# Query scores in a fused agent attention: agents as fp32 weights, softmax by 32x32 turns on VectorE

## The chip, the cores and the metric

The kernel runs on one core of one Trainium2 chip. The metric is the time of one execution in microseconds (us), the median of several runs. Besides these, one execution was recorded by the hardware profiler; all rows shown are from it. Engines are TensorE (PE in the profile, with PEld its weight loads), VectorE (DVE), ScalarE (ACT), GpSimd (POOL) and SyncE (SP, which issues DMAs).

## The reference

Four batches of 12480 tokens with 128 channels, 49 agents per batch, then a gated feed-forward layer with 2048 hidden columns over all 49920 tokens:

```python
def sm(a, b):
    s = scale * (a @ b.transpose(0, 2, 1))
    s = s - s.max(-1, keepdims=True)
    e = np.exp(s)
    return e / (e.sum(-1, keepdims=True) + 1e-09)
a2k = sm(agents, k)          # 49 x 12480 per batch
agent_v = a2k @ v            # 49 x 128
q2a = sm(q, agents)          # 12480 x 49
x = (q2a @ agent_v)          # 12480 x 128
h = x @ w_in                 # 128 -> 2048
out = (h * (1 / (1 + np.exp(-1.702 * h)))) @ w_out
```

The weights of the feed-forward layer come as float64.

## The kernel before

`agent_v @ w_in` is worked out once per batch, so that the up product of a token is its 49 softmax values times a 49 x 2048 matrix (`wh`, `wl`: the high part in fp32r and the rest). The tokens go in 52 **groups** of 960 (`GT`), 13 a batch; a group is held as two halves of 480 tokens, half c on the partitions from 64c on. For a group there are 16 **chunks** of 128 hidden columns (`NF`). A chunk has three pairs of up matmuls (`up`, L538: wh x q_hi, wh x q_lo, wl x q_hi, one of each pair per row tile of 64 rows), a gelu on ScalarE (L558), the high part gh of it (by a GpSimd DMA for even chunks and chunks 1 and 9, else on ScalarE), the rest gl on VectorE (`low`, L575), and six pairs of down matmuls (`down`, L580), in two rounds of three, since each row tile adds to both output banks `po`. All of these go through `half_matmul` (L209), where two row tiles run side by side.

The order on every engine is written out by hand. A group is 17 **gaps** (`GAPS`); each gap first runs the jobs put into it (`at[t]`, in the order of the `put` calls), then the up pairs of a chunk (six chunks ahead of its down matmuls), then gl of the chunk three before that, then the second down round of one chunk and the first of the next. Gap 1 has no up pairs (L1039), so that 17 gaps hold 16 chunks. At the end of a group `store` (L603) copies the two output banks out: both halves on ScalarE for the first five groups of the first three batches, else one on ScalarE and one on VectorE.

The next group's softmax stands in these gaps (L902 to L917). Before them, in gaps 12 to 15 of the group before, VectorE splits q into three bf16 parts (`split`, L185, four pieces). In gaps 0 and 1 `scores` (L230) multiplies them with bf16 parts of the agents, 16 pairs of small matmuls a run, tokens as weights, with the two runs swapping the banks of `ps_m`; the result has 120 tokens on the partitions. In gap 2 `query_shift` (L461) adds two sums, takes the maximum and subtracts it; gap 4 has the exp on ScalarE (with a table load before and after), gap 6 the sums and the product (L486, L492), gap 8 the transposes of `query_pairs` (L501) on TensorE, from which ScalarE and VectorE make q_hi and q_lo.

Keys and values of the next batch take slots in the same gaps (L939 on): key scores at gaps 4, 10 and 13 of a group, each with four split pieces before it and a store on ScalarE and VectorE after it; values at gaps 12 and 6, each with a DMA, a subtraction (L369), a sum (L391) and a pair of operations on e (L361). `ps_m` is one buffer of two PSUM banks, shared by all of them.

The start (`start`, L784) handles the first batch's keys and values in fp32, with the first two groups' scores (`scores_exact`) and their softmax between the steps of the key softmax on VectorE; then `first_weights` (L400) copies the accumulated values and the first up matmuls follow. Its value matmuls (`first_values`, L763) are fp32 on column tiles: 49 weights of 64 columns, at `tile_position=(0, c * H)`.

Of the kernel before, what the change touches and what calls it, by code (L numbers as in the profile page):

```python
# [17 lines left out]
P = 128  # L18
# [11 lines left out]
Z_AT = 6  # L30
P_AT = 8
# [10 lines left out]
def kernel(  # L42
# [31 lines left out]
    ag_sb = const.tile([P, B, A], F32, name="ag_sb")  # L74
    nc.sync.dma_start(out=ag_sb, in_=agT)
# [19 lines left out]
    p_pad = const.tile([P, CH // TB, P], F32, name="p_pad")  # L95
    nc.gpsimd.memset(p_pad, 0.0)


    e_sb = const.tile([P, KB, A + 1], F32, name="e_sb")
    nc.gpsimd.memset(e_sb[:, :, A:], EPS)  # L100
# [70 lines left out]
    rest = ag_sb  # L171
# [84 lines left out]
    def scores_exact(b, x, out):  # L256

        for j in range(KB):
            nc.tensor.matmul(
                out=out(j), lhsT=x[:, j * TB : (j + 1) * TB], rhs=ag_sb[:, b, :], start=True, stop=True  # L260
            )
# [22 lines left out]
    def first_key_scores(g, kt):  # L284

        for c in range(2):
            ps = ps_h.tile([P, 512], F32, name="ph")
            for j in range(KB // 2):
                nc.tensor.matmul(  # L289
                    out=ps[:TB, j * 2 * A : (j + 1) * 2 * A],  # L290
                    lhsT=kt[:, c * KB // 2 + j, :],
                    rhs=ag_sb[:, 0:2, :].rearrange("p b a -> p (b a)"),
                    start=True,
                    stop=True,
                )
# [160 lines left out]
    def query_load(b, g):  # L456
        t = loads.tile([P, GT + PAD], F32, name="qt", tag="qt", bufs=1)
        nc.sync.dma_start(out=t[:, 0:GT], in_=qT[b, :, g * GT : (g + 1) * GT])
        return t

    def query_shift(s):  # L461

        m = work.tile([P, KB], F32, name="m")
        sd = e_sb[:TB, :, 0:A]
        if isinstance(s, tuple):
            nc.scalar.copy(out=by_bank(sd), in_=s[0])
            nc.vector.tensor_add(out=by_bank(sd), in0=s[1], in1=by_bank(sd))
            s = [by_bank(sd)]
        mb = m[:TB].rearrange("p (c j) -> p c j", c=2)
        at = 0  # L470
        for bank in s:
            c = slice(at, at + bank.shape[1])
            at = c.stop
            nc.vector.tensor_reduce(out=mb[:, c], in_=bank, axis=AX.X, op=ALU.max)
            nc.vector.tensor_tensor(
                out=by_bank(sd)[:, c],
                in0=bank,
                in1=mb[:, c].unsqueeze(3).broadcast_to([TB, c.stop - c.start, KB // 2, A]),
                op=ALU.subtract,
            )  # L480
        return sd
# [4 lines left out]
    def query_sums(n):  # L486
        z = work.tile([P, KB], F32, name="z")
        nc.vector.tensor_reduce(out=z[:TB], in_=e_sb[:TB], axis=AX.X, op=ALU.add)
        nc.vector.reciprocal(out=z[:TB], in_=z[:TB])
        return z  # L490

    def query_softmax(n, e, z):  # L492
        pp = p_pad
        nc.vector.tensor_tensor(
            out=pp[:TB].rearrange("p i (c x) -> p c i x", c=2)[:, :, :, 0:A],
            in0=e.rearrange("p (c i) a -> p c i a", c=2),
            in1=z[:TB].rearrange("p (c i) -> p c i", c=2).unsqueeze(3).broadcast_to([TB, 2, KB // 2, A]),
            op=ALU.mult,
        )

    def query_pairs(g):  # L501
        pp = p_pad
        ps = two_banks()
        q_hi = work.tile([P, CH], F32R, name="q_hi")
        q_lo = work.tile([P, CH], F32R, name="q_lo")
        r = slice(0, H + A)
        rows = [slice(0, H), slice(H, TB)]
        for i in range(CH // TB):
            for c, t in enumerate(rows):
                n = t.stop - t.start  # L510
                half_matmul(
                    (ps.name, c),
                    c,
                    out=ps[:, c, i * n : (i + 1) * n],
                    lhsT=pp[t, i, :],
                    rhs=ident[t, t],
                    start=True,
                    stop=True,
                    is_transpose=True,
                )  # L520

        def piece(q, c):
            t = rows[c]
            return q[r].rearrange("p (i t) -> p i t", t=TB)[:, :, t]

        def scored(c):
            n = rows[c].stop - rows[c].start
            return ps[r, c, : CH // TB * n].rearrange("p (i t) -> p i t", t=n)

        for c in range(2):  # L530
            nc.scalar.copy(out=piece(q_hi, c), in_=scored(c))
        for c in range(2):
            nc.vector.tensor_sub(out=piece(q_lo, c), in0=scored(c), in1=piece(q_hi, c).bitcast(F32))
# [92 lines left out]
    q_parts = {}  # L626
# [32 lines left out]
    def do_query_split(n, i):  # L659
        if n in exact:  # L660
            q_parts[n] = qts.pop(n, None) or q_parts[n]
        elif n < B * NG:
            if i == 0:
                q_parts[n], pieces[n] = split(qts.pop(n))
            pieces[n](i)

# [14 lines left out]
    def do_key_sum(b, g):  # L681
        if g == 0:
            accs[b] = work.tile([P, 2, 2 * C + 1], F32, name="acc")
        key_sum(g, sums.pop((b, g)), accs[b])

    def do_query_scores(n, c):
        if n < B * NG:
            if c == 0:
                banks[n] = score_banks() if n in exact else wide_banks()
            if n not in exact:  # L690
# [430 lines left out]
```

## Time and profile before

| | |
|---|---|
| median of three runs | 1903.03 us (1902.35 to 1903.81) |
| the profiled execution's span, first to last instruction | 1901.8 us |
| TensorE busy | 1887.1 us (99%) |
| VectorE busy | 1547.8 us (81%) |
| ScalarE busy | 1431.9 us (75%) |
| GpSimd busy | 327.7 us (17%) |
| chain of waits that ended last, by engine | PE 86%, issue 7%, DMA 2%, DVE 2% |

The span is that of the profiled execution; the runs' times lie about 1.2 us above it. Matmuls overlap, so their durations add up to more than the time that they take: what a stretch of them costs is read from the starts of its neighbours. In a row such as `128x480 f32<-128x480 f32` the first shape is the output, the second the input.

### The profile page before, as it was taken

The numbers are of one execution on the slowest core, as the hardware profiler recorded it, in microseconds if no ns is written. First come the engines' busy times: TensorE is split into PE (matmuls) and PEld (weight loads), VectorE is DVE, ScalarE is ACT, GpSimd is POOL, SyncE is SP. The second block draws the span as 40 slices with busy tenths as digits, with TensorE's granted clock in tenths as the row PEclk, the third lists the DMA queues.
The fourth block names the chain that finished last, engine by engine and source line by source line (L and its number), as shares of the span: only waits on it lengthen the run. The fifth ranks groups of instructions, "written<-read, shape, count | busy, mean of one in ns | idle before, by whom it ended". The sixth has DMA issues, their size and how long they took to land.

```text
span 1901.8 us, 53518 instructions
## 1 busy us (share of the span) xinstructions
PE 1887.1 (99%) x22152; PEld 1767.2 (93%) x22152; DVE 1547.8 (81%) x2042; ACT 1431.9 (75%) x2480; POOL 327.7 (17%) x671
## 2 busy tenths in 40 slices
PE   8999999999999999999999999999999999999999
PEld 8799999999899999999988999999898999999998
DVE  7888889788789888888878898888887777777775
ACT  4777777778777777777777777877777878778785
POOL 0111112222111111222211111222211111111111
PEclk9999999999999999999999999999999999999999
DMA  9566478888566657978856655999984555555453
GB/s 355 181 204 204 167 215 227 223 231 231 165 202 216 199 170 221 224 225 231 220 166 215 197 187 175 222 228 227 224 207 153 191 174 178 178 185 179 168 185 137
DMA packets 158863, 384.57 MB, mean 202 GB/s; under 512 B 15683, under 2 KB 73219, under 8 KB 158619
## 3 DMA queue, kind: packets, MB, share of 16 engines
q0 software_dynamic: 115008, 273.33, 48.0%
q1 hardware_dynamic: 43611, 107.83, 19.8%
q8 instruction: 173, 2.83, 0.7%
q14 instruction: 71, 0.58, 0.1%
HBM read 82.25 MB, written 25.56 MB: 57 GB/s over the span
## 4 chain that ended last, share of the span: by engine, by line
PE 86%; issue 7%; DMA 2%; DVE 2%; POOL 1%; ACT 1%; SPq 0%; POOLq 0%; DVEq 0%; ACTq 0%
PE po L213 49%; PE ph L213 26%; PE ps_m L213 7%; DMA gh<-g 2%; PE ph L289 1%; DVE gl L577 1%; PE ps_m L425 1%; POOL gh L570 1%; DMA vt<-v 1%; PE po L599 0%; ACT g L558 0%; POOL v_pair L365 0%; PE po L769 0%; DMA kt<-kT 0%; ACT L558 0%
## 5 line engine op out<-in xcount | busy, mean ns | idle before, releaser
L558 ACT ACTIVATE g<-ph 128x480 f32<-128x480 f32 x1664 | 853.7, 571 | 372.7 <-PE ph L213 359.9
L577 DVE TENSOR_TENSOR gl<-g,gh 128x960 fp32r<-128x960 f32 x832 | 940.0, 1153 | 170.4 <-DMA gh<-g 136.9
L213 PE MATMUL po<-gh,wo_h 64*128 64x480 f32 x3300 | 795.1, 380 | 2.7 <-SPq L220 2.7
L213 PE MATMUL po<-gl,wo_h 64*128 64x480 f32 x3300 | 788.4, 377 | 0.1
L213 PE MATMUL po<-gh,wo_l 64*128 64x480 f32 x3300 | 787.4, 376 | 0.0
L570 POOL DMA_DIRECT2D gh<-g x517 | 275.9, 534 | 1521.8 <-ACT g L558 1275.8
L213 PEld LDWEIGHTS po<-gh,wo_h 64*128 64x128 f32 x3300 | 464.3, 184 | 20.1 <-ACT o L607 4.3
L213 PEld LDWEIGHTS po<-gl,wo_h 64*128 64x128 f32 x3300 | 465.5, 186 | 13.4 <-DVE gl L577 1.5
L213 PEld LDWEIGHTS po<-gh,wo_l 64*128 64x128 f32 x3300 | 463.5, 184 | 12.7
L213 PE MATMUL ph<-q_hi,wh 49*128 49x480 f32 x1664 | 417.8, 400 | 1.0 <-ACT g L558 0.8
L213 PE MATMUL ph<-q_lo,wh 49*128 49x480 f32 x1664 | 397.3, 377 | 0.0
L213 PE MATMUL ph<-q_hi,wl 49*128 49x480 f32 x1664 | 395.6, 376 | 0.0
L572 ACT CAST gh<-g 128x960 fp32r<-128x960 f32 x312 | 312.7, 1002 | 8.3
L213 PEld LDWEIGHTS ph<-q_hi,wh 49*128 49x128 f32 x1664 | 233.7, 185 | 21.3 <-ACT g L558 9.2
L213 PEld LDWEIGHTS ph<-q_hi,wl 49*128 49x128 f32 x1664 | 232.6, 184 | 7.8 <-DVE wl L431 0.6
L213 PEld LDWEIGHTS ph<-q_lo,wh 49*128 49x128 f32 x1664 | 233.5, 187 | 4.9
L213 PE MATMUL ps_m<-ag_part,rest 64*128 64x98 bf16 (+1 forms) x2816 | 135.9, 192 | 0.1
L194 DVE TENSOR_TENSOR rest<-rest 128x488 bf16<-128x488 f32 (+1 forms) x176 | 127.3, 724 | 0.0
L213 PEld LDWEIGHTS <-rest 64*128 64x128 bf16 x2816 | 122.7, 94 | 0.3
L213 PE MATMUL ps_m<-ag_part,qt 64*128 64x98 bf16 (+1 forms) x1600 | 81.3, 195 | 0.0
L213 PEld LDWEIGHTS <-qt 64*128 64x128 bf16 x1600 | 66.9, 93 | 14.0 <-issue 9.2
L609 DVE COPY o<-po 128x480 f32<-128x480 f32 x37 | 24.3, 658 | 56.7 <-PE po L213 51.2
(130 smaller groups left out, 1331.8 us busy)
## 6 DMA issues: line engine op xcount, KB each, us to landing
gh<-g POOLq DMA_DIRECT2D x517, 480.0 KB, 3.8
kt<-kT SPq DMA_DIRECT2D x52, 480.0 KB, 4.1
outT<-o SPq DMA_DIRECT2D x104, 240.0 KB, 4.8
qt<-qT SPq DMA_DIRECT2D x50, 480.0 KB, 4.2
vt<-v SPq DMA_DIRECT2D x39, 512.0 KB, 4.7
v_pair<-vt POOLq DMA_DIRECT2D x39, 480.0 KB, 6.6
vt<-v SPq DMA_DIRECT2D x13, 480.0 KB, 4.8
words<-w_in SPq DMA_DIRECT2D x4, 512.0 KB, 8.7
```

What stands on the lines that cost most here:

```text
L194: nc.vector.tensor_sub(out=halves(r)[1][:, s], in0=r[:, s], in1=halves(r)[0][:, s])
L213: ins = nc.tensor.matmul(tile_position=(c * H, 0), **kw)
L289: nc.tensor.matmul(out=ps[:TB, j * 2 * A : (j + 1) * 2 * A], lhsT=kt[:, c * KB // 2 + j, :], rhs=ag_sb[:, 0:2, :].rearrange("p b a -> p (b ...
L425: nc.tensor.matmul(out=out, lhsT=w["avT"], rhs=w_in_sb[:, s], start=True, stop=True)
L558: nc.scalar.activation(out=g[:, c, :], in_=ph[c][:, :CH], func=AF.Gelu_apprx_sigmoid)
L570: nc.gpsimd.dma_start(out=gh, in_=g)
L572: nc.scalar.copy(out=gh, in_=g)
L577: nc.vector.tensor_sub(out=gl, in0=g, in1=gh.bitcast(F32))
L609: nc.vector.tensor_copy(out=o, in_=po[c][:, :CH])
```

## The change

The scores of a group are made with the agents as weights, in fp32: four matmuls, 64 weights (49 agents, then 15 of them again) by 240 tokens, two on each of two column tiles; agents then lie on the partitions and tokens stream. VectorE turns the result in blocks of 32x32, so that a token's 64 values lie in two blocks on two sets of 32 partitions; it takes maximum and sums over both (`other_agents` copies the neighbour's small tile across), and turns back after the product. The splits of q, the second run, the pads and the transposes on TensorE go. Gap 0 is now the one without up pairs, and sums, product and q_hi, q_lo stand in gaps 5, 6 and 7.

```diff
-Z_AT = 6
-P_AT = 8
+Z_AT = 5
+P_AT = 6
+R_AT = 7
+BL = 32
...
+    ag_raw = gpool.tile([P, B, A], F32, name="ag_raw", tag="gl", bufs=GL_BUFS)
+    nc.sync.dma_start(out=ag_raw, in_=agT)
+    ag_sb = const.tile([P, B, H], F32, name="ag_sb")
+    nc.vector.tensor_copy(out=ag_sb[:, :, 0:A], in_=ag_raw)
+    nc.vector.tensor_copy(out=ag_sb[:, :, A:], in_=ag_raw[:, :, BL : BL + H - A])
...
+    def query_scores(b, x, ps):
+        n = CH // 2
+        for i in range(2):
+            for c in range(2):
+                t = c * CH + i * n
+                nc.tensor.matmul(
+                    out=ps[c * H : (c + 1) * H, i * n : (i + 1) * n],
+                    lhsT=ag_sb[:, b, :],
+                    rhs=x[:, t : t + n],
+                    start=True,
+                    stop=True,
+                    tile_position=(0, c * H),
+                )
+    def other_agents(t):
+        x = work.tile([P, CH // BL], F32, name="x", bufs=1)
+        for i in range(0, P, BL):
+            to = i ^ BL
+            nc.vector.tensor_copy(out=x[to : to + BL], in_=t[i : i + BL])
+        return x
+    def query_turn(ps):
+        e = work.tile([P, CH], F32, name="e")
+        nc.vector.transpose(out=e, in_=ps[:, :CH])
+        return e
+    def query_shift(e):
+        m = work.tile([P, CH // BL], F32, name="m", bufs=1)
+        nc.vector.tensor_reduce(out=m, in_=blocks(e), axis=AX.X, op=ALU.max)
+        x = other_agents(m)
+        nc.vector.tensor_tensor(out=m, in0=m, in1=x, op=ALU.max)
+        nc.vector.tensor_tensor(out=blocks(e), in0=blocks(e), in1=per_block(m), op=ALU.subtract)
+    def query_sums(e):
+        n = A - BL
+        z = work.tile([P, CH // BL], F32, name="z", bufs=1)
+        r = work.tile([P, CH // BL], F32, name="r", bufs=1)
+        nc.vector.tensor_reduce(out=z, in_=blocks(e)[:, :, 0:n], axis=AX.X, op=ALU.add)
+        nc.vector.tensor_reduce(out=r, in_=blocks(e)[:, :, n:BL], axis=AX.X, op=ALU.add)
+        nc.vector.scalar_tensor_tensor(out=z, in0=r, scalar=low_rows[:, 0:1], in1=z, op0=ALU.mult, op1=ALU.add)
+        x = other_agents(z)
+        nc.vector.scalar_tensor_tensor(out=z, in0=x, scalar=EPS, in1=z, op0=ALU.add, op1=ALU.add)
+        nc.vector.reciprocal(out=z, in_=z)
+        return z
+    def query_softmax(e, z):
+        nc.vector.tensor_tensor(out=blocks(e), in0=blocks(e), in1=per_block(z), op=ALU.mult)
+        p = work.tile([P, CH], F32, name="p", tag="e")
+        nc.vector.transpose(out=p, in_=e)
+        return p
+    def query_pairs(p):
+        q_hi = work.tile([P, CH], F32R, name="q_hi")
+        q_lo = work.tile([P, CH], F32R, name="q_lo")
+        nc.scalar.copy(out=q_hi, in_=p)
+        nc.vector.tensor_sub(out=q_lo, in0=p, in1=q_hi.bitcast(F32))
         return q_hi, q_lo
...
         if n:
-            for i in range(4):
-                put(t - 5 + i, lambda m=m, i=i: do_query_split(m, i))
-            take(t, 2)
-            put(t, lambda m=m: do_query_scores(m, 0))
-            put(t + 1, lambda m=m: do_query_scores(m, 1))
-            put(t + 2, lambda m=m: do_query_shift(m))
+            take(t, 1)
+            put(t, lambda m=m: do_query_scores(m))
+            put(t + 1, lambda m=m: do_query_turn(m))
             put(t + E_AT, lambda m=m: do_query_exp(m))
             put(t + Z_AT, lambda m=m: do_query_sums(m))
-            put(t + Z_AT, lambda m=m: do_query_softmax(m))
-        take(t + P_AT, 1)
-        put(t + P_AT, lambda m=m: do_query_pairs(m))
+            put(t + P_AT, lambda m=m: do_query_softmax(m))
+        put(t + R_AT, lambda m=m: do_query_pairs(m))
...
-        elif n == 0 and k < 2:
-            u = LAG - 1 + k
         elif final:
             u = n * NF + LAG + k
-        elif k == 1:
-            u = None
+        elif k == 0:
+            u = LAG - 1 if n == 0 else None
         else:
-            u = n * NF + LAG + max(k - 1, 0)
+            u = n * NF + LAG + k - 1
```

`do_query_turn` runs `query_turn` and `query_shift` one after the other. In the start the calls stay where they were: the scores of both groups by `query_scores`, their shift, sums and product by the new functions.

## Rows read from the trace of the kernel before

**Rows 1.** The page's busy time of each engine: us, share of the span, instructions.
```profile
PE 1887.1 (99%) x22152; PEld 1767.2 (93%) x22152; DVE 1547.8 (81%) x2042; ACT 1431.9 (75%) x2480; POOL 327.7 (17%) x671
```

**Rows 2.** Key, value, plain group: length, PE PEld DVE ACT POOL busy, clock, DMA.
```profile
1000.79:1038.09 37.30, 37.28 (x554) 33.33 (x553) 33.65 (x48) 27.64 (x49) 5.78 (x14) 1.00 0.61 199
423.27:458.31 35.04, 35.04 (x396) 34.53 (x393) 29.03 (x37) 27.16 (x47) 7.37 (x14) 1.00 0.86 228
1603.45:1636.63 33.18, 33.18 (x363) 30.84 (x360) 24.32 (x29) 26.15 (x46) 5.96 (x12) 1.00 0.53 180
```

**Rows 3.** Timeline of TensorE around both score runs: start, us, line, output<-input, count.
```profile
1603.24 0.56 PE L213 MATMUL po<-gh,wo_l 64*128 64x480 f32 x2
...
1604.40 0.49 PE L213 MATMUL ph<-q_lo,wh 49*128 49x480 f32 x2
...
1605.28 0.48 PE L213 MATMUL po<-gh,wo_l 64*128 64x480 f32 x2
...
1606.38 0.49 PE L213 MATMUL po<-gl,wo_h 64*128 64x480 f32 x2
```

**Rows 4.** Timeline of TensorE around the transposes, and ten steady pairs after.
```profile
1619.14 0.57 PE L213 MATMUL po<-gh,wo_l 64*128 64x480 f32 x2
...
1619.88 0.57 PE L213 MATMUL ph<-q_lo,wh 49*128 49x480 f32 x2
...
1622.05 0.58 PE L213 MATMUL ph<-q_hi,wl 49*128 49x480 f32 x2
```

**Rows 5.** Timeline of TensorE: fp32 on column tiles, and one full-array fp32 matmul.
```profile
33.06 4.61 PE L769 MATMUL po<-vt,score 120*49 120x129 f32 x80
...
49.07 1.09 PE L769 MATMUL po<-vt,score 120*49 120x129 f32 x16 [0.41 <-DMA vt<-v]
...
72.61 0.38 PE L213 MATMUL po<-gh,wo_l 64*128 64x480 f32 x2
72.92 1.12 PE L425 MATMUL ps_m<-w_in_sb,avT 128*128 128x512 f32 x2
...
74.30 0.38 PE L213 MATMUL ph<-q_lo,wh 49*128 49x480 f32 x2
```

**Rows 6.** VectorE's groups by line and shape: count, busy us, mean ns, idle before.
```profile
L194 DVE TENSOR_TENSOR rest<-rest 128x488 bf16<-128x488 f32 x88 | 64.0, 727 | 0.0
...
L474 DVE TENSOR_REDUCE m<-e_sb 120x8 f32<-120x392 f32 x50 | 28.1, 562 | 1.7
...
L609 DVE COPY o<-po 128x480 f32<-128x480 f32 x37 | 24.3, 658 | 56.7 <-PE po L213 51.2 <-PE po L599 5.3
...
L489 DVE RECIPROCAL z<-z 120x8 f32<-120x8 f32 x52 | 10.6, 203 | 1.8
...
L173 DVE CAST ag_part<-ag_sb 128x196 bf16<-128x196 f32 x1 | 1.8, 1795 | 1.8 <-DMA ag_sb<-agT 1.8
```

**Rows 7.** Timeline of the start: the first key scores, VectorE's first and last query work.
```profile
5.42 22.73 PE L289 MATMUL ph<-ag_sb,kt 128*120 128x98 f32 x208 [0.17 <-DMA kt<-kT]
...
33.04 0.56 DVE L474 TENSOR_REDUCE m<-ps_m 120x8 f32<-120x392 f32 x1
...
46.98 0.57 DVE L494 TENSOR_TENSOR p_pad<-e_sb,z 120x392 f32<-120x392 f32 x1
50.19 0.29 DVE L402 COPY both<-po 128x130 f32<-128x130 f32 x1 [2.65 <-PE po L769]
```

**Rows 8.** Timeline after a group's end: the output's copies and the first down weights.
```profile
1038.55 1.03 ACT L607 COPY o<-po 128x480 f32<-128x480 f32 x2
...
1039.63 0.18 PEld L213 LDWEIGHTS po<-gh,wo_h 64*128 64x128 f32 x1 [0.27 <-ACT o L607]
```

**Rows 9.** Timeline of a value group: gl of chunk 9, and its first use.
```profile
442.10 1.16 DVE L577 TENSOR_TENSOR gl<-g,gh 128x960 fp32r<-128x960 f32 x1 [3.20 <-DMA gh<-g]
443.18 0.72 DVE L533 TENSOR_TENSOR q_lo<-ps_m,q_hi 113x256 fp32r<-113x256 f32 x2
...
443.77 0.46 PE L213 MATMUL po<-gl,wo_h 64*128 64x480 f32 x2
```

More of the change, by code (lines that the diff above doesn't have):

```diff
@@ L259, in scores_exact @@
             nc.tensor.matmul(
-                out=out(j), lhsT=x[:, j * TB : (j + 1) * TB], rhs=ag_sb[:, b, :], start=True, stop=True
+                out=out(j), lhsT=x[:, j * TB : (j + 1) * TB], rhs=ag_sb[:, b, 0:A], start=True, stop=True
             )
@@ L456, in query_load @@
     def query_load(b, g):
-        t = loads.tile([P, GT + PAD], F32, name="qt", tag="qt", bufs=1)
-        nc.sync.dma_start(out=t[:, 0:GT], in_=qT[b, :, g * GT : (g + 1) * GT])
-        return t
[L461 to L481, printed above, removed]
+        t = loads.tile([P, GT], F32, name="qt", tag="qt", bufs=1)
@@ new lines, in query_load @@
+        nc.sync.dma_start(out=t, in_=qT[b, :, g * GT : (g + 1) * GT])
+        return t
+    def query_scores(b, x, ps):
+        n = CH // 2
+        for i in range(2):
+            for c in range(2):
+                t = c * CH + i * n
[7 more added lines that the diff above has]
+                )
@@ L522, in piece @@
[L522 to L533, printed above, removed]
+        nc.scalar.copy(out=q_hi, in_=p)
@@ L625 @@
     k_parts = {}
-    q_parts = {}
     scored = {}
@@ L657, in do_key_split @@
         pieces[b, g](i)
[L659 to L665, printed above, removed]
     def do_key_scores(b, g, c):
@@ L682, in do_key_sum, with do_query_scores, do_query_turn @@
         if g == 0:
-            accs[b] = work.tile([P, 2, 2 * C + 1], F32, name="acc")
+            accs[b] = work.tile([P, 2, 2 * C + 1], F32, name="acc", bufs=1)
         key_sum(g, sums.pop((b, g)), accs[b])
-    def do_query_scores(n, c):
+    def do_query_scores(n, ps=None):
         if n < B * NG:
-            if c == 0:
-                banks[n] = score_banks() if n in exact else wide_banks()
-            if n not in exact:
-                scores(n // NG, q_parts[n], banks[n][0], c, True)
-            elif c == 0:
-                scores_exact(n // NG, q_parts[n], columns(banks[n][0]))
-    def do_query_shift(n):
+            banks[n] = two_banks()[:, 0] if ps is None else ps
+            query_scores(n // NG, qts.pop(n), banks[n])
+    def do_query_turn(n):
         if n < B * NG:
-            s = banks.pop(n)[1]
-            scored[n] = query_shift(s if isinstance(s, (list, tuple)) else [s])
+            scored[n] = query_turn(banks.pop(n))
+            query_shift(scored[n])
     def do_query_exp(n):
@@ L705, in do_query_sums @@
         if n < B * NG:
-            sums[n] = query_sums(n)
+            sums[n] = query_sums(scored[n])
     def do_query_softmax(n):
         if n < B * NG:
-            query_softmax(n, scored.pop(n), sums.pop(n))
+            scored[n] = query_softmax(scored[n], sums.pop(n))
     def do_query_pairs(n):
         if n < B * NG:
-            pairs[n] = query_pairs(n)
+            pairs[n] = query_pairs(scored.pop(n))
     def first_keys():
@@ L810, in start @@
                     steps.pop(0)()
-        banks[0] = score_banks()
-        scores_exact(0, qts.pop(0), columns(banks[0][0]))
+        do_query_scores(0)
         d = {}
@@ L818, in start @@
         key_max_2(d, ps_h.tile([P, 512], F32, name="ph"))
-        halves1 = [ps_h.tile([P, 512], F32, name="ph") for _ in range(2)]
-        scores_exact(0, qts.pop(1), lambda j: halves1[j // 4][:TB, j % 4 * A : (j % 4 + 1) * A])
-        banks[1] = None, [
-            t[:TB, : KB // 2 * A].rearrange("p (c j a) -> p c j a", c=1, a=A) for t in halves1
-        ]
+        do_query_scores(1, ps_h.tile([P, 512], F32, name="ph"))
         for g in range(NKG):
@@ L885, in gap_of @@
         n, k = divmod(u - LAG, NF)
-        return LAG + n * GAPS + (k + 1 if k else 0)
+        return LAG + n * GAPS + k + 1
     def put(t, fn):
```

51 lines of the change are left out of this document (11 added, 40 removed).

## The prediction

> **What bounds the kernel now.** I read the busy times first. TensorE is busy 1887.1 us of 1901.8 [rows 1]; the other engines have room. Then three groups cut out of the steady part, each from the start of one group's query scores to the next [rows 2]: one in which the next batch's keys are scored (three key runs), one in which keys meet values, one with neither. [...] The reader is to see two things: time taken from TensorE's stream is time gained, and VectorE has little left in the key groups. By the code there are 39 key tiles after the first batch, scored three a group, and 39 value tiles, two a group: some 13 key groups and 20 value groups of 52.
>
> **Part 1: TensorE's stream.** A steady pair of row-tile matmuls takes 0.217 us: ten pairs from 1619.88 to 1622.05 [rows 4]. What a query run costs is the time between the pair before and the pair after, less one pair. First run: 1603.24 to 1604.40 holds one pair of wo_l, the run, one pair of q_hi whose second start is late: 1.16 - 0.43 = 0.73. Second run: 1605.28 to 1606.38, 1.10 - 0.43 = 0.67. Transposes of the finished softmax: 1619.14 to 1619.88, 0.74 - 0.43 = 0.31 [rows 3, 4]. Together 1.71. The other way round, the group's 33.18 us less 144 pairs (16 chunks of nine) is 33.18 - 31.25 = 1.93, which holds a few small hitches as well. I take 1.75 removed per group.
>
> Added: four fp32 matmuls of 240 columns, two on each column tile, each of which runs as two passes. The nearest rows are the start's value matmuls, fp32 on the same two column tiles [rows 5]: 80 passes take 4.61 us and 16 take 1.09, so 64 passes take 3.52, or 0.110 for two passes of 129 columns; that is 0.853 ns a column for two passes. The full-array fp32 matmul below needs 1.25 us for 1024 columns of one pass, so at 0.43 ns a column and pass the two tiles can only run side by side. Eight passes of 240 columns are four such steps of 0.205, 0.82 us. The change of tile shape costs more: a 512-column fp32 matmul between row-tile pairs, 72.61 to 74.30, takes 1.69 - 0.43 = 1.26, of which its two passes at 0.853 ns are 0.87; 0.39 are edges. With weights half as wide the edges are somewhat shorter; I take 0.35. New run: 1.17 (bounds 1.05 to 1.30 with tiles side by side, 2.0 if they are not). Gain 1.75 - 1.17 = 0.58 a group, times 50 groups, 29.0; the transposes of the second group, which has its scores in the start, add 0.3. **Minus 29.3** (bounds minus 38 and minus 22).
>
> **Part 2: the cover of the output banks.** The new group's first down matmul waits until the last group's output has been copied out of its two banks. Where ScalarE does both copies (groups 0 to 4 of the first three batches, 15 times) it begins at 1038.55, 0.46 after the group's start at 1038.09, and the second bank's weight load goes at 1039.63, 0.27 late: 1.54 after the start [rows 8]. Now the run is followed by that down matmul at once, since the gap has no up matmuls: TensorE is there at 1.17 and not at about 1.3. It waits some 0.2 longer, 15 times: **plus 3** (0 to 6). In the other groups one copy is on VectorE and both are done near 1.0, which the run just covers.
>
> **Part 3: VectorE.** Removed per group: four split pieces of at most 0.73, five passes of 392 columns at 0.56, a reciprocal of 0.20, two subtractions of some 0.8 together: 6.6. Added [rows 6]: by 562 ns for 392 columns and 658 for 480 an operation costs 1.09 ns a column and 0.13. Turn, maximum and subtraction of the shift are 0.66 each, with four copies of 15 columns and one maximum of two small tiles: the trace has 0.20 for 8 columns where the operation waits for the one before (L489), and neighbours that don't wait overlap by 0.08 (442.10 + 1.16 against 443.18 [rows 9]), which would make it 0.1; I take 0.2 for each since every such chain begins and ends with a wait: 3.0. Sums: 0.41 + 0.38 for 17 and 15 of 32 columns, four copies and three more small ones: 2.2. Softmax and turn back 1.4, q_lo 0.66. Together 7.2 us, 0.6 more than before. The trace has no turn on VectorE: 0.66 is what an operation of 480 columns out of PSUM takes (L609), and twice that is the other bound.
>
> [...]
>
> [...]
>
> *In the start* VectorE is the bound. Its work from the first query operation at 33.04 to the last, ending at 47.55, is without a pause; then it is idle 2.65 us before it copies the accumulated values at 50.19, from which the first weights, and with them every up matmul, follow [rows 7]. All of both groups' query work stands ahead of that copy. Per group it is now some 3.3 and will be 7.2: 2 x 3.9 = 7.8, less the 2.65: **plus 5.2** (3.3 to 7.8). The new copies of the agents ahead of the first key scores are hidden: the agents land at about 2.75, even a copy as slow as the cast there (1.80) and a second of 0.2 end by 4.8, and the first key tile lands only at 5.4 [rows 6, 7].
>
> *In the steady part* the order counts, since each gl must be there when its down pair comes. Gaps without other work last 1.95 (nine pairs); a gap's first wo_h pair of chunk f needs gl three gaps after it was issued, seven pairs into the gap. Counted from the scores' start: gap 0 is 1.17 + 0.65, so chunk 3 is wanted at 7.2. VectorE can begin the turn at 1.4, ends the shift at 4.4, then a key piece of 0.7 and gl of chunk 3, done at 6.3: in time by 0.9, where before it came ahead of the shift. Going on with 1.1 a gl and 0.7 a piece, the sums end at 12.8, the softmax at 15.2, key store and piece at 16.9, gl of chunk 8 at 18.0 (wanted 18.3), of chunk 9 at 20.3 (wanted 20.3). After that no query split stands in gaps 12 to 15 any more and VectorE catches up. So a key group stalls by nothing to half a microsecond; I take 0.1. In a value group the tight one is chunk 9, today held by its DMA and not by VectorE's load: 3.20 us idle until 442.10, done at 443.26, used at 443.77 [rows 9], a slack of 0.5. TensorE will be there 0.58 + 0.3 earlier, the DMA only by the 0.3 that the stream gains ahead of it: 0.1 late from that alone, and if VectorE's own backlog counts (two gl, 3.0 shift, 0.9 key pair, 2.2 sums, 1.4, then q_lo, key sum and pair ahead of chunk 9) about 1.0 late. I take 0.4 of these. 13 x 0.1 + 20 x 0.4: **plus 9.3** (0 to 33, a full microsecond in each of the 33).
>
> ScalarE loses a copy and gains nothing of size. Its q_hi now comes one gap earlier and waits for VectorE's turn back; I cost that at nothing because the exp in gap 4 puts ScalarE itself behind at that point. If that cover is gone it waits up to a gap, and TensorE has two chunks of ph ahead of it to go on with. GpSimd loses 50 memsets of pads. The key slots, the loads and the gap in which exp stands are as before.
>
> **Sum.** 1901.85 - 29.3 + 3 + 5.2 + 9.3 = 1890.0. The median of the runs, 1903.03, lies 1.2 above the span; with it 1891.2.
>
> **The rivals.**
> - *VectorE is never late.* The small copies cost 0.1, chunk 9's DMA moves with the stream: the 9.3 go and half of part 2. 1880. For it: VectorE is idle 3.6 us even in the key group, and the added work is only 0.6. Against: the work moves into the first seven gaps.
> - *VectorE becomes the bound in key and value groups* (the other side). Place: the gl behind shift, sums and softmax. Price: if a turn takes 1.3 rather than 0.66 and a small copy 0.3, the chain up to chunk 9 is 2.1 longer (0.64 twice and 0.1 eight times), so the 33 groups lose some 1.9 each, 63 us instead of 9.3: 1945. It decides from a loss of (29.3 - 5.2 - 3) / 33 = 0.64 us per group on. For it: idle time of 3.65 and no slack by my own count. Against: gl catches up in each group's last gaps.
> - *The column tiles run one after the other*, because both take 128 rows. The run is 2.0, 0.25 worse than what it replaces: 1903.0 + 12.2 + 5.2 + 3 = 1923. Against it stand the start's matmuls at 120 rows [rows 5].
>
> **How the numbers follow.** Forecast 0.50, VectorE never late 0.25, VectorE the bound 0.15, tiles in turn 0.05, else 0.05. A measurement of this kernel can tell 0.2%, 3.8 us, from no change. The forecast's own bounds run from 1871 to 1926 if all terms go one way; three quarters of its chance is below 1899, an eighth within. Faster: 0.375 + 0.25 + 0.02 = 0.65; same 0.10; slower 0.25. The range 1874 to 1912 reaches into the first rival whole and leaves the far part of the others out; the likeliest case alone is 1880 to 1903.
>
> **What would show it.** Score pass pairs 0.2 us apart and a run of 1.1 to 1.2 between pairs; a plain group of 32.6 us against 33.18; the copy of the accumulated values near 55.4 in place of 50.19; VectorE's turn at 0.66; TensorE waiting for gl in the gaps 8 to 10 of value groups. Wrong if the run is over 1.5, if a turn is over 1 us, or if ScalarE is seen waiting for the turn back for more than a microsecond a group.

## The result and the profile after

The changed kernel takes 1929.88 us (median of 4 runs, 1926.15 to 1930.66), the kernel before 1903.42 on the same chip: ratio 1.0133, 95% interval 1.0119 to 1.0147. It is slower by 1.3%; the prediction, 1891.2 with a range of 1874 to 1912, has the wrong sign. The profiled execution has a span of 1928.7 us against 1901.8.

The page of the changed kernel, busy time of each engine (answers to [rows 1]) and its chain that ended last, by engine:

```profile
PE 1886.9 (98%) x18920; PEld 1658.0 (86%) x18920; DVE 1576.5 (82%) x2468; ACT 1417.8 (74%) x2378; POOL 320.9 (17%) x623
...
PE 68%; DVE 14%; issue 8%; ACT 3%; DMA 2%; POOL 1%; SPq 0%; POOLq 0%; DVEq 0%; ACTq 0%
```

TensorE is busy for as long as before (1887.1), in a span that is 26.9 longer: it now waits. VectorE, which had 2% of the chain before, has 14%. The groups of the changed kernel, from one score run to the next (answers to [rows 2]): a key group, two value groups, a plain group; length, then busy PE, PEld, DVE, ACT, POOL, clock, DMA:

```profile
146.06:184.28 38.22, 37.37 (x491) 33.11 (x489) 33.81 (x55) 27.68 (x48) 5.63 (x13) 1.00 0.60 194
437.91:473.80 35.89, 34.89 (x329) 31.16 (x329) 29.89 (x45) 26.74 (x45) 7.06 (x13) 1.00 0.90 221
368.00:402.97 34.97, 34.97 (x330) 31.93 (x329) 29.62 (x45) 26.83 (x45) 7.35 (x13) 1.00 0.81 229
1599.42:1632.44 33.02, 33.02 (x297) 28.86 (x296) 24.73 (x37) 25.82 (x44) 4.76 (x9) 1.00 0.51 176
```

The plain group is 0.16 shorter than in [rows 2], not 0.58; the key group is 0.9 longer and TensorE stands idle in it for 0.85. I cut the whole steady part of both profiles into groups in this way. Mean lengths before and after, and what the difference adds to:

| stretch | before | after | in all |
|---|---|---|---|
| start, up to the first steady score run | 98.64 | 107.91 | +9.3 |
| 12 key groups | 37.24 | 38.36 | +13.4 |
| 5 groups with the end of a key phase | 35.15 | 36.11 | +4.8 |
| 18 value groups | 35.30 | 35.35 | +0.9 |
| 3 groups after a change of weights | 38.01 | 38.46 | +1.3 |
| 11 plain groups | 33.21 | 33.02 | -2.1 |
| the rest to the end | 65.85 | 65.18 | -0.7 |

What TensorE waits for in the changed kernel (engine, line, releaser: us in total, times, longest):

```profile
PE ps_m L216 <- DVE rest L197: 13.2, 26, 1.4
...
PE ps_m L412 <- DVE both L405: 2.7, 1, 2.7
...
PE po L216 <- DVE gl L575: 1.5, 4, 0.5
```

The largest wait is for `rest` of L197, the last split piece of a key tile: twice in each key group. For gl, whose due times the prediction worked out, its matmuls wait next to nothing; its weight loads, which stand ahead of them, come with e5 below.

### The profile page after: what moved, and what is told of

Same layout as the page of the kernel before. It is cut to its first block, busy times and chain, and to the rows that moved or that the text cites. A ratio compares the mean times of both kernels' runs of the same rounds, so it can differ in the third digit from the quotient of the medians.

```text
span 1928.7 us, 47298 instructions
## 1 busy us (share of the span) xinstructions
PE 1886.9 (98%) x18920; PEld 1658.0 (86%) x18920; DVE 1576.5 (82%) x2468; ACT 1417.8 (74%) x2378; POOL 320.9 (17%) x623
## 4 chain that ended last, share of the span: by engine, by line
PE 68%; DVE 14%; issue 8%; ACT 3%; DMA 2%; POOL 1%; SPq 0%; POOLq 0%; DVEq 0%; ACTq 0%
PE po L216 41%; PE ph L216 21%; DVE gl L575 6%; PE ps_m L216 3%; DMA gh<-g 2%; DVE rest L197 2%; PE ps_m L470 1%; ACT g L556 1%; DVE rest L195 1%; DVE x L490 1%; POOL gh L568 1%; DVE score L314 1%; DVE q_lo L531 1%; DVE m L500 0%; PE po L597 0%
## 5 line engine op out<-in xcount | busy, mean ns | idle before, releaser
L216 PE MATMUL po<-gh,wo_h 64*128 64x480 f32 x3300 | 815.6, 381 | 4.1 <-SPq L223 4.0
L216 PE MATMUL po<-gl,wo_h 64*128 64x480 f32 x3300 | 805.9, 377 | 1.7 <-DVE gl L575 1.5
L216 PE MATMUL po<-gh,wo_l 64*128 64x480 f32 x3300 | 802.8, 376 | 0.0
L216 PE MATMUL ph<-q_hi,wh 49*128 49x480 f32 x1664 | 424.6, 391 | 3.7 <-ACT g L556 3.4
L216 PE MATMUL ph<-q_lo,wh 49*128 49x480 f32 x1664 | 411.2, 380 | 0.0
L216 PE MATMUL ph<-q_hi,wl 49*128 49x480 f32 x1664 | 406.3, 376 | 0.0
L216 PE MATMUL ps_m<-ag_part,rest 64*128 64x98 bf16 x1216 | 60.4, 192 | 13.2 <-DVE rest L197 13.2
L216 PEld LDWEIGHTS <-rest 64*128 64x128 bf16 x1216 | 51.2, 94 | 16.6 <-DVE rest L197 16.3
L216 PE MATMUL ps_m<-ag_part,kt 64*128 64x98 bf16 x1216 | 62.9, 195 | 0.0
```

The lines of the kernel that those rows point to most:

```text
L216: ins = nc.tensor.matmul(tile_position=(c * H, 0), **kw)
```

## The experiments

Times are medians beside the kernel before on the same chip; ratios with their 95% interval are to that. Group lengths are means over the groups of the table above, from each run's trace. The start of one and the same program differs by up to 1.7 us between executions (107.9 in the changed kernel, 108.5 and 109.6 in e4 and e3, whose start is not edited), so differences of the start below 2 us are not read.

| run | time | ratio | start | key | key end | value | plain |
|---|---|---|---|---|---|---|---|
| changed | 1929.9 | 1.0133 [1.0119, 1.0147] | 107.9 | 38.36 | 36.11 | 35.35 | 33.02 |
| e1 warm | 1924.8 | 1.0116 [1.0100, 1.0131] | 106.3 | 38.29 | 35.70 | 35.35 | 33.02 |
| e2 start | 1926.5 | 1.0122 [1.0108, 1.0136] | 104.6 | 38.30 | 36.36 | 35.32 | 33.02 |
| e3 keys | 1913.4 | 1.0063 [1.0050, 1.0075] | 109.6 | 37.21 | 36.32 | 35.24 | 33.02 |
| e4 gap 0 | 1932.3 | 1.0156 [1.0142, 1.0170] | 108.5 | 38.24 | 35.74 | 35.34 | 33.39 |
| e5 no copies | 1902.1 | 0.9996 [0.9987, 1.0005] | 104.9 | 37.22 | 35.36 | 34.85 | 33.02 |
| e6 no exp | 1919.2 | 1.0084 [1.0069, 1.0100] | 107.7 | 38.31 | 36.34 | 35.29 | 32.65 |
| e7 = e1+e2+e3 | 1911.4 | 1.0043 [1.0030, 1.0055] | 102.4 | 37.18 | 36.18 | 35.36 | 33.02 |
| e8 = e7, maximum later | 1903.2 | 1.0004 [0.9995, 1.0013] | 103.7 | 37.15 | 35.11 | 35.31 | 33.02 |
| e9 = e8, DMA for chunk 7 | 1902.3 | 1.0001 [0.9992, 1.0010] | 101.6 | 37.12 | 35.09 | 35.24 | 33.02 |
| e10 = before, DMA for chunk 7 | 1903.7 | 1.0006 [0.9997, 1.0015] | 97.9 | 37.25 | 35.16 | 35.33 | 33.21 |
| e11 = e9, sums later | 1901.9 | 0.9996 [0.9987, 1.0004] | 103.2 | 37.19 | 35.10 | 35.16 | 33.02 |
| e12 = e11, no exp | 1895.3 | 0.9960 [0.9946, 0.9973] | 102.2 | 37.31 | 35.12 | 35.09 | 32.65 |
| e13 = e11, output copy | 1904.3 | 1.0011 [1.0002, 1.0020] | 101.6 | 37.58 | 34.88 | 35.08 | 33.03 |

**The key groups: order or load (e3, e5).** In the changed kernel, VectorE in the first gaps of the key group that starts at 107.91, then TensorE at its key scores of gap 4 (start, us, engine and line, output<-input, shape, count):

```profile
109.56 0.68 DVE L495 STREAM_TRANSPOSE e<-ps_m 128x480 f32<-128x480 f32 x1
...
110.95 0.70 DVE L490 COPY x<-m 32x15 f32<-32x15 f32 x4
...
111.90 0.66 DVE L503 TENSOR_TENSOR e<-e,m 128x480 f32<-128x480 f32 x1
112.48 0.73 DVE L197 TENSOR_TENSOR rest<-rest 128x488 bf16<-128x488 f32 x1
113.09 1.16 DVE L575 TENSOR_TENSOR gl<-g,gh 128x960 fp32r<-128x960 f32 x1
...
114.72 1.16 DVE L575 TENSOR_TENSOR gl<-g,gh 128x960 fp32r<-128x960 f32 x1
115.79 0.70 DVE L197 TENSOR_TENSOR rest<-rest 128x480 bf16<-128x480 f32 x1
```

```profile
116.54 0.20 PE L216 MATMUL ps_m<-ag_part,rest 64*128 64x49 bf16 x1 [0.27 <-DVE rest L197]
```

The shift ends 4.65 after the group's start (4.4 predicted) and gl follows at 6.3, as predicted; but the last piece is done only at 8.6, and the scores that start at 7.9 want it at 8.4. In most key groups TensorE waits about 0.4 here and as long again at the scores of gap 10. Edit of e3:

```diff
+            ahead = 5 if b or k > 2 else 4
             for i in range(4):
-                put(t - 4 + i, lambda b=b, k=k, i=i: do_key_split(b + 1, k, i))
+                put(t - ahead + i, lambda b=b, k=k, i=i: do_key_split(b + 1, k, i))
```

> The changed kernel with the four split pieces of each key tile one gap earlier (all but the first three tiles). Theory A (order: in a key group TensorE waits some 0.4 us at the scores of gap 4 and again at those of gap 10 for a split piece that stands behind turn, shift and sums on VectorE): these waits go, key groups fall from 38.2 to some 37.1 us, 12 groups and the ends of the key phases with them, time 1929.9 - 13 = 1917. Rival B (load: VectorE has too much to do in gaps 1 to 9, whatever the order): the wait moves to gl, key groups stay at 38 us, 1928 to 1931.

Edit of e5, in `other_agents`:

```diff
-            nc.vector.tensor_copy(out=x[to : to + BL], in_=t[i : i + BL])
-        return x
+            pass
+        return t
```

> The changed kernel without the eight small copies of a group that exchange maximum and sum between the two 32-row halves (left out of the computation: maximum and sum then go over one half of the agents). It takes 8 x 0.17 = 1.4 us a group off VectorE and changes no order. Theory A (VectorE's queue ahead of the split pieces, of which order is one part and length another): the turn and shift are 0.7 shorter, so the wait of 0.4 at gap 4 goes, that at gap 10 shrinks; key groups 37.2 to 37.6 instead of 38.2; the start is 2.7 shorter; 1929.9 - 11 - 3 = 1915 to 1918. Rival B (the length of VectorE's work is not what holds the key groups, only the order): key groups 38.2, 1927. Plain groups 33.02 by both.

In the key groups e3 came out as theory A said, to the tenth (37.2 for 37.1): the waits for `rest` are gone, but for one of 0.3, and a later key group of that run is without idle time, with VectorE as busy as in the changed kernel:

```profile
582.20:619.33 37.13, 37.13 (x491) 33.59 (x489) 33.87 (x55) 27.79 (x48) 5.62 (x13) 1.00 0.61 201
```

So the order alone is worth 1.15 a key group. The ends of the key phases, which I had expected to fall with them, do not (36.32). And e5, which keeps the order and takes 1.4 us off VectorE, does the same for the key groups, and saves 0.5 in each value group and 0.75 at each end of a key phase as well: 28 us where I expected 12 to 15. Both theories are right of a queue that is late by some half a microsecond. What e5 adds is that value groups, in which no split piece stands, are held by VectorE too, in two ways by gl. First, TensorE's weight loads wait for it; in the changed kernel and in e5:

```profile
PEld po L216 <- DVE gl L575: 6.2, 12, 0.9
```

```profile
PEld po L216 <- DVE gl L575: 0.2, 1, 0.2
```

Second, and for more of the 0.5, ScalarE waits for it, since a gelu's output `g` takes a buffer that an earlier gl must have read. ScalarE's wait in all, then in the value group that starts at 402.97 in the changed kernel; behind it the same of e5, group start 391.81:

```profile
ACT g L556 <- DVE gl L575: 17.3, 32, 1.8
...
409.76 1.03 ACT L556 ACTIVATE g<-ph 128x480 f32<-128x480 f32 x2 [0.20 <-DVE gl L575]
410.81 1.28 ACT L506 ACT_TABLE_LOAD   x1
```

```profile
ACT g L556 <- DVE gl L575: 4.0, 7, 1.0
...
398.30 1.03 ACT L556 ACTIVATE g<-ph 128x480 f32<-128x480 f32 x2
399.35 1.28 ACT L506 ACT_TABLE_LOAD   x1
```

The table load for the exp comes 7.84 after the group's start and not 7.54. This wait stands at some 7 us in each of the 18 value groups of the changed kernel and in none of e5, and by it the up matmuls that need ScalarE's next bank of ph start later, in most groups by 0.30 (12.89 for 12.59). That is more than half of the 9.0 us that the value groups give back.

**The start (e1, e2).** VectorE in the changed kernel: the copy of the accumulated values, which the prediction put at 55.4, and the first gh; behind it the first gh of the kernel before, whose copy came at 50.19 [rows 7]. Then the granted clock (last but two columns) of the stretches before and behind:

```profile
55.59 0.26 DVE L405 COPY both<-po 128x130 f32<-128x130 f32 x1
...
62.28 0.66 DVE L566 CAST gh<-g 128x960 fp32r<-128x960 f32 x1 [0.99 <-ACT g L556]
```

```profile
54.52 0.66 DVE L568 CAST gh<-g 128x960 fp32r<-128x960 f32 x1 [0.35 <-ACT g L558]
```

```profile
47.00:52.00 5.00, 4.19 (x46) 4.12 (x48) 4.74 (x10) 4.74 (x9) 0.00 (x0) 0.66 0.42 150
52.00:55.00 3.00, 1.21 (x22) 0.95 (x18) 2.75 (x12) 0.12 (x1) 0.00 (x0) 1.00 0.46 161
55.00:62.00 7.00, 6.09 (x24) 4.45 (x24) 3.09 (x9) 1.73 (x4) 0.00 (x0) 0.53 0.01 2
```

The copy is where VectorE's queue puts it. TensorE however has two pauses of 2.5 and 2.7 us, and behind each the granted clock falls to half (0.51 from 50 to 52 us, 0.50 from 56 to 62): the stretch with the first weights is at 0.53, and from the copy to the first gh it takes 6.7 us where the kernel before, at 1.00 throughout, took 4.3. Edits:

```diff
 # e1: in the loop over value matmuls, and behind it
+            if g == 9:
+                keep_warm(10)
...
+        keep_warm(11)
         first_weights(w0)
 # e2: out of the start, into the first group's gaps (q_hi and q_lo from gap 7 to 9)
-                do_query_sums(1)
-                do_query_softmax(1)
...
+        else:
+            put(t + 5, lambda m=m: do_query_sums(m))
+            put(t + 6, lambda m=m: do_query_softmax(m))
```

> The changed kernel with 21 dummy 128-column fp32 matmuls on TensorE in the two pauses of the start (10 before the tenth group of value matmuls, 11 behind the last), no other edit. Theory A (the pauses of 2.5 and 2.7 us let the granted clock fall to 0.50, and the first weights run at half clock): the granted clock stays 1.00 from 45 to 64 us, the stretch from the copy of the accumulated values to the first gh of VectorE is 4.3 us as in the kernel before and not 6.7, the first steady group begins 2.4 us earlier, time near 1927.5. Rival B (that stretch is longer because VectorE and ScalarE have other work in it): stretch and time unchanged, 1929.9. If the dummies stand in the way of the first weights, 1931.

> The changed kernel with the sums and the softmax of the second group (3.6 us on VectorE) taken out of the start and put into gaps 5 and 6 of the first group, its q_hi and q_lo two gaps later. Theory A (the start is longer by VectorE's queue ahead of the copy of the accumulated values, plus the clock's fall behind it): the copy is at 52.0 us and not at 55.6, the pause before it is too short for the clock to fall, the first steady group begins 5 to 6 us earlier, less what VectorE then lacks in the first group's gaps (0 to 2): 1924 to 1927. Rival B (VectorE is the bound of the whole stretch up to 85 us, so the same work later costs the same): the copy is earlier, the first steady group is not, 1929 to 1931.

e1: the first pause is filled (clock 1.00 from 47 to 52), the second still has 1.6 us and the clock behind it 0.75; the stretch is 5.7, one of the 2.4 us. But neither can be put down to the dummies: in e4 (below), whose start is not edited, the clock happens to stay at 1.00 from 47 to 52 too, and the stretch is 5.88:

```profile
47.00:52.00 5.00, 3.81 (x64) 3.45 (x64) 4.75 (x11) 4.82 (x9) 0.00 (x0) 1.00 0.49 166
55.51:61.39 5.88, 5.57 (x25) 3.68 (x26) 2.50 (x10) 2.02 (x5) 0.00 (x0) 0.71 0.01 3
```

The intervals of e1's ratio and the changed kernel's overlap as well, so e1 settles nothing. That the stretch goes with the clock is shown by all runs together: in the nine in which the clock is at 1.00 in it (the kernel before, e2, e7 to e13) it takes 4.32 or 4.33, in the six others, at 0.5 to 0.7, from 5.7 to 6.7. e2's VectorE, and TensorE's wait 25 us later:

```profile
52.40 0.29 DVE L405 COPY both<-po 128x130 f32<-128x130 f32 x1 [0.97 <-PE po L754]
...
56.72 0.66 DVE L566 CAST gh<-g 128x960 fp32r<-128x960 f32 x1 [0.34 <-ACT g L556]
```

```profile
PE ph L216 <- DVE wl L434: 2.3, 1, 2.3
```

The stretch is 4.32, with the clock at 1.00. But the moved sums and softmax now stand ahead of the low halves of the weights (L434), for which TensorE waits 2.3 at 81.1 (granted clock behind it, from 81 to 83, 0.50); A in the start, B behind it.

**The cover of the output banks (e4).** Edit, beside the same in `gap_of`:

```diff
+        elif n == 0 and k < 2:
+            u = LAG - 1 + k
...
-        elif k == 0:
-            u = LAG - 1 if n == 0 else None
+        elif k == 1:
+            u = None
         else:
-            u = n * NF + LAG + k - 1
+            u = n * NF + LAG + max(k - 1, 0)
```

> The changed kernel with the up matmuls back in gap 0, between the score run and the first down matmul, and none in gap 1, as in the kernel before. Theory A (part 2 of the prediction: without up matmuls there the first down matmul waits for the output banks, some 0.2 us in the 16 groups in which ScalarE makes both copies): these groups lose the wait and nothing else changes, 1926 to 1927. Rival B (the gl of the gap is also issued earlier, so VectorE is late less often): key groups fall by more, 1922. Rival C (it doesn't matter, the wait is hidden by the lag between the two row tiles): 1929.9.

None of the three. The wait that theory A names is gone (in the 15 groups with both copies on ScalarE the fourth matmul behind the run starts 1.50 after its beginning, not 1.75). But plain groups are 0.37 longer (value groups are not). TensorE of this run in such a group, at the border of gaps 0 and 1:

```profile
1600.90 0.38 PE L216 MATMUL po<-gh,wo_l 64*128 64x480 f32 x2
1601.38 0.48 PE L216 MATMUL po<-gh,wo_h 64*128 64x480 f32 x2
1601.69 0.38 PE L216 MATMUL po<-gl,wo_h 64*128 64x480 f32 x2
```

0.48 and 0.31 in place of 0.22 twice. By the code, the two halves of chunk 0's down product swap their banks between the row tiles, and with no up matmuls between, each tile must wait for the other's last write. Before the change the second score run stood there. So, in these runs, putting the up matmuls into gap 1 costs 0.25 in 15 groups and saves 0.37 in each plain group.

**The plain groups (e6, e9, e10).** TensorE of the changed kernel around a score run (answers to [rows 3]):

```profile
1631.91 0.37 PE L216 MATMUL po<-gh,wo_l 64*128 64x480 f32 x1
1631.92 0.37 PE L216 MATMUL po<-gl,wo_h 64*128 64x480 f32 x1
1632.14 0.38 PE L216 MATMUL po<-gh,wo_l 64*128 64x480 f32 x1
1632.44 1.03 PE L470 MATMUL ps_m<-qt,ag_sb 128*64 128x240 f32 x8
1633.40 0.49 PE L216 MATMUL po<-gh,wo_h 64*128 64x480 f32 x2
1633.73 0.39 PE L216 MATMUL po<-gl,wo_h 64*128 64x480 f32 x2
```

The eight passes go in pairs and the run costs what was predicted: from the last start ahead, 1632.14, to the second pair behind, 1633.73, less two pairs of 0.217, 1.16. But the last start ahead stands alone. One row tile is a pair behind the other, and the run, on all 128 rows, has to wait for it: 0.21 more. That lag was there before the change (in [rows 3] the second start of the pair at 1603.24 is 0.18 behind the first), and there the score runs, on half the rows, let each tile go on by itself: one starts its scores at 1603.45, the other at 1603.64. It arises in gap 6 (my expectations say gap 5), where TensorE needs a bank of ph that ScalarE has not read yet (in the group below its weight load at 1611.25 waits 0.28 for g); ScalarE in a plain group of the changed kernel:

```profile
1605.91 1.03 ACT L556 ACTIVATE g<-ph 128x480 f32<-128x480 f32 x2
1606.95 1.28 ACT L506 ACT_TABLE_LOAD   x1
1608.25 0.60 ACT L506 ACTIVATE e<-e 128x480 f32<-128x480 f32 x1
1608.87 1.28 ACT L556 ACT_TABLE_LOAD   x1
1610.16 2.42 ACT L556 ACTIVATE g<-ph 128x480 f32<-128x480 f32 x5
```

Edit of e6, in `query_exp`:

```diff
-        nc.scalar.activation(out=e, in_=e, func=AF.Exp, scale=scale)
+        nc.scalar.mul(out=e, in_=e, mul=0.0)
```

> The changed kernel with a multiplication by zero on ScalarE in place of the queries' exp (the exp is left out of the computation), so that a plain group has no table load on ScalarE. Theory A (the plain group gives back its gain because ScalarE, held by two table loads of 1.3 us around the exp, lets TensorE's two row tiles get out of step by one pair of 0.21 us in gap 5, and the new score run, which needs all rows, has to wait for the late tile): the hitch of 0.2 in gap 5 goes and the score run is 0.2 shorter, plain groups 32.6 instead of 33.02. Rival B (the lag of one tile comes from elsewhere, or costs nothing): only the hitch goes, 32.8, and the last two starts ahead of the score run stay 0.21 apart. Rival C (neither): 33.0.

Theory A, to 0.05: plain groups 32.65, and the run starts 0.32 behind two tiles that are in step:

```profile
1625.97 0.39 PE L216 MATMUL po<-gh,wo_l 64*128 64x480 f32 x2
1626.29 1.03 PE L470 MATMUL ps_m<-qt,ag_sb 128*64 128x240 f32 x8
```

I then tried to take the lag away without leaving the exp out, by a cast of 1.0 us less on ScalarE ahead of it, in the best combination (e9) and in the kernel before (e10):

```diff
-        return u > EARLY and (f % 2 == 0 or f in BY_DMA)
+        return u > EARLY and (f % 2 == 0 or f in BY_DMA or f == 7 and not 6 <= u // NF % 13 < 12)
```

> The last combination (pieces earlier, start lighter, maximum later; 1903.2), with the gh of chunk 7 by DMA instead of ScalarE's 1.0 us cast in gap 2, in the 34 groups that have no value matmuls. Theory A (ScalarE, one us earlier at the exp of gap 4, has its table loads done before TensorE needs the ph banks again, so the tiles stay in step): plain groups 32.65 as without the exp, 34 groups x 0.37 = 12.6, time 1891. Rival B (the DMA brings gh later than ScalarE did, gl of chunk 7 is late): plain groups over 33.0, 1903 to 1910.

> The kernel before with the same edit (gh of chunk 7 by DMA in the same 34 groups). Theory A (there the lag costs nothing at the score runs, which take half the rows each; only the hitch in gap 5 of 0.15 goes): plain groups 33.07, 34 x 0.15 = 5, time 1898. Rival B (the lag costs the same there): 33.22 - 0.37 = 32.85, 1890. Rival C (gh late): 1903 or more.

Both missed: plain groups stay at 33.02 and 33.21. In e9 ScalarE simply waits longer for TensorE before each g (first row), so the exp starts where it did, right behind the g of gap 3:

```profile
1574.92 1.03 ACT L556 ACTIVATE g<-ph 128x480 f32<-128x480 f32 x2 [0.93 <-PE ph L216]
1575.97 1.28 ACT L506 ACT_TABLE_LOAD   x1
```

So the lag comes from the 3.2 us of two loads and the exp, not from the cast ahead of them. The edit of e9 shortens only the three groups after a change of weights, by 0.86 each.

**What the losses add up to (e7, e8, e11, e12, e13).** e7 takes e3, e1 with 10 and 2 dummies, and e2 two gaps later:

```diff
-            put(t + 5, lambda m=m: do_query_sums(m))
-            put(t + 6, lambda m=m: do_query_softmax(m))
+            put(t + 7, lambda m=m: do_query_sums(m))
+            put(t + 8, lambda m=m: do_query_softmax(m))
```

e8 moves the transposes of the keys' maximum:

```diff
-        t = free(t + 3)
+        t = free(t + 4)
         put(t, lambda mx=mx: key_max_1(mx))
-        t = free(t + 2)
+        t = free(t + 3)
```

> The changed kernel with split pieces one gap earlier, the second group's sums and softmax in gaps 7 and 8 of the first group (behind the weights' parts that stood behind them in gaps 5 and 6) with q_hi and q_lo in gap 9, and dummy matmuls in the start (10 and 2). Theory A (the three losses are apart and add up): key groups 37.2, the first steady group begins near 102 instead of 107.9, 1929.9 - 13.5 - 5.5 = 1911. Rival B (the first group's VectorE backlog takes the gain of the start back): 107, 1916. It does not reach the kernel before (1902.3) by either, since plain groups gain 0.2 and not 0.58.

> The same, with the two transposes of the keys' maximum one gap later each. Theory A (at the end of each key phase TensorE waits 0.7 to 2.1 us in a gap for VectorE's maximum, three times): 1911 - 3 to 5 = 1907. Rival B (the wait is only moved, or the later shift of the values' exponents takes it back): 1911.

Both are theory A: the parts add up, and the ends of the key phases fall by 1.07, to the length before the change. (Of the 8 us between the two medians the profiled executions show 5.3.) With that the loss is gone, and nothing gained. e11, on top of e9:

```diff
-Z_AT = 5
-P_AT = 6
-R_AT = 7
+Z_AT = 6
+P_AT = 7
+R_AT = 8
```

> The first of these three with sums, softmax and q_hi/q_lo one gap later (6, 7 and 8). Theory A (in value groups the gl of chunk 9 is late because VectorE makes sums and softmax ahead of it): the stall of 0.5 some 21 us into a value group goes where it stands, 0.2 to 0.5 in 18 groups, 1891 - 6 = 1885. Rival B (chunk 9 waits for its DMA, not for VectorE's load): 1891. Rival C (q_lo comes too late for the next group's first up matmul in gap 11, or key pieces are late again): over 1891.

Value groups fall by 0.08 only, a miss for A. But B, by which chunk 9 waits for its DMA, is not shown either: ScalarE's wait for gl at 7 us, ahead of the sums wherever they stand, is in all 18 value groups of this run as well. Two runs then asked where the predicted gain is missing: e12, e11 with e6's edit, and e13, e11 with one output copy on VectorE in every group:

```diff
-            if c == 0 or g < 5 and b < B - 1:
+            if c == 0:
```

> The last combination (1901.9) with a multiplication by zero on ScalarE in place of the queries' exp (the exp is left out of the computation). With VectorE's order mended, what the tiles' lag costs should show in the key groups too. Theory A (lag and hitch cost 0.37 in every group without key exponents, 34 of them): plain 32.65, key groups 36.8 to 36.9, 1901.9 - 12.6 = 1889, which is what the prediction had summed up to. Rival B (key groups have no lag to lose, their last two starts are 0.05 apart; they are held by VectorE): only plain groups and the three after a weights' change gain, 1901.9 - 4 - 1.3 = 1896.5.

> The last combination (1901.9) with one of the two output copies on VectorE in every group (the exp is back). Theory A (in the 15 groups in which ScalarE makes both, the second tile's first down matmul starts 0.46 later and the fourth start of the group 0.26 later): fourth start at 1.50 after the score run and not 1.75, 15 x 0.26 = 4, 1898. Rival B (VectorE's 0.66 in the key groups comes ahead of the turn and makes split pieces or gl late again): key groups over 37.4, 1902 to 1906.

B in both. Without the exp plain groups again give 0.37, key groups nothing. In e13 VectorE reaches its copy so late that in the key groups it ends 1.36 after the score run's start, where ScalarE's second copy ended too; TensorE waits for split pieces again (4.9 us in 12 waits), and those groups are 0.4 longer. No version is faster than the kernel before beyond its interval, except e12, which leaves the exp out.

## Why the prediction was wrong

- *What bounds the kernel*: TensorE had no idle time to give, and VectorE little in key groups. Right, and the second half should have been followed up.
- *Part 1, minus 29.3*: the run (1.16 against 1.17) and what it replaces (1.72 against 1.75) were right. Mis-sized was the difference in the stream: the run waits 0.21 for the late row tile, the hitch of gap 6 is 0.05 larger and the other pairs take 0.2185 for 0.2177, 0.09 a group. Plain groups gain 0.19, a third of 0.58. What failed here is the reading of [rows 3] as time between pairs, without asking whether both tiles end together.
- *Part 2, plus 3*: right in place and size, 0.25 in 15 groups. That the same move saves 0.37 in a plain group at the border of gaps 0 and 1 I had not seen; it hid the cost of taking the second run away.
- *Part 3, durations*: right. Turns, subtraction and copies of the changed kernel (count, busy, mean ns, idle before):

```profile
L524 DVE STREAM_TRANSPOSE p<-e 128x480 f32<-128x480 f32 x52 | 35.3, 679 | 1.8
...
L490 DVE COPY x<-m 32x15 f32<-32x15 f32 x208 | 34.8, 167 | 3.9
L495 DVE STREAM_TRANSPOSE e<-ps_m 128x480 f32<-128x480 f32 x51 | 34.4, 675 | 1.2 <-PE ps_m L470 1.2
L503 DVE TENSOR_TENSOR e<-e,m 128x480 f32<-128x480 f32 x52 | 34.2, 658 | 1.8
```

  The turns take 0.679 and 0.675, some 0.02 more than the subtraction of 480 columns (0.658); the copies take 0.17 each and four of them 0.70, with no overlap.
- *Part 3, the start, plus 5.2*: the copy came at 55.59 (55.4 predicted). It measured plus 9.3. The prediction has two terms at nothing: TensorE's granted clock falls to 0.50 behind the wait that this makes (2.4 us), and VectorE's backlog goes on into the first group. There it reaches TensorE by way of SyncE, in a pause of 1.4 at 86.6 which the kernel before does not have: the relay (L223) that orders the two tiles' writes to a bank stands in SyncE's queue behind a key load, and that load waits for VectorE's wo_l until 87.5:

```profile
SPq L284 <- DVE wo_l L169: 3.4, 1, 3.4
```

- *Part 3, the steady part, plus 9.3*: this is the step that failed most. I compared gl with its due time, chunk by chunk, and wrote that the key slots are as before. Their split pieces stand in the same queue, and I never compared them with theirs: 0.4 us late twice in a key group, 1.1 longer groups where I had summed 0.28 shorter ones, some 17 of the 39 us between forecast and measurement. The maximum at the end of the key phases is the same mistake (4.8 longer than before; e8 takes it away). No single step turned the sign: with the order of the pieces mended (e3) the kernel is still 0.6% slower, and it is level only with start and maximum mended too (e8). The 0.4 that I took for a value group is near the 0.5 that e5 gives back, but by luck: I had put it on chunk 9 at 20 us, and more than half of it is ScalarE's wait for a gl at 7 us.
- *The rivals*: nearest is VectorE as the bound in key and value groups, at 0.15. Its price (a slower turn) was wrong, and its place (gl) holds in value groups alone; in key groups it is the split pieces. None of the signs of being wrong that the prediction lists came (run 1.16, turn 0.68, ScalarE's wait for the turn back 7.8 us in the whole run), since none of them looked at the key pieces. The column tiles do run side by side; the score passes start in pairs 0.20 apart. The prediction's own bounds, added up again with the 1.2, are 1868 to 1928 and not 1871 to 1926; 1929.9 lies beyond them.

Still open is why key groups do not fall to 36.9 once their order is mended. Lag and hitch are not it (e12). In e3 TensorE's weight loads wait 0.3 for the gl of chunk 9, at some 20.8 us of 11 of the 12 key groups, but in e5, where they do not, key groups are as long. And the copy to VectorE that should have tested the output banks came too late to do so (e13).

## What to carry to other kernels

When work moves into a queue that is nearly full, write down the due time of everything behind it in that queue, not only of the operand that seemed tight: here 3 us of softmax delayed a split piece by 0.4, twice a group, and that was the largest part of the loss. Ask the same of a buffer that the moved work frees late, and of the engine that waits for it. An operation on all rows is a meeting point for row tiles that are out of step; a run that replaces half-row runs must be charged with their lag, here 0.21 in a plain group. And before work is moved out from between two matmuls, look for what it kept apart, such as a bank that the two write in turn. Where moved work makes TensorE pause, look at the granted clock behind the pause: here it was 0.50 behind both pauses in the start of the changed kernel, and the stretch from the copy to the first gh took 6.7 us for 4.3.

## What the runs showed of the hardware

- Two row tiles of TensorE went on independently: in the rows of the changed kernel above, the later product of one tile starts at 1631.91, 0.01 before the earlier product of the other. The score run starts 0.30 behind the last product ahead of it, and the next pair 0.30 behind its last pass. What makes these 0.30 at both edges, in place of 0.22 between pairs, no run here shows.
- A pause of TensorE was followed by a lower granted clock in some places and not in others. Behind those of 2.5 and 2.7 us in the start of the changed kernel it was 0.51 (50 to 52 us) and 0.50 (56 to 62), behind that of 2.3 in e2 0.50 (81 to 83). In e4, whose start is the same program, it was 1.00 behind the first pause (47 to 52) and 0.71 behind the second, there some 4 us long (55.51 to 61.39). Behind the pause of 1.6 in the start of e1 it was 0.50 (57 to 58); behind those of 1.6 in the first group of the kernel before (71 to 74) and of the changed kernel (77.3 to 82) it was 1.00.
- A table load of ScalarE took 1.28 us; exp and g follow theirs within 0.02, so that nothing beyond the 1.28 shows.
